# Thirty-six steps of unread identity products on TensorE, and a new written order, in a one-core gated-loop attention kernel with an MLP behind it

## The chip, the cores and the metric

The kernel runs on one core of one Trainium2 chip. The metric is the device time in microseconds of one execution. Inputs lie in the device's memory before the kernel starts, and the output is written there. The core has five engines that each execute their own instructions in order: TensorE (PE in the profile; its weight loads are counted apart, as PEld), VectorE (DVE), ScalarE (ACT), GpSimd (POOL) and SyncE (SP), which here only issues the transfers.

## The reference

Four batches, eight heads, 768 tokens, 48 channels. Each token decays a complex state per channel, adds an outer product of key and value, and is read with the query. The result is put side by side over the heads (3072 tokens of 384 values) and goes through an MLP of 2048 features with a parametric ReLU.

```
B, H, S, D = 4, 8, 768, 48
mag = sqrt(a_re*a_re + a_im*a_im);  scale = minimum(mag, 0.999) / (mag + 1e-6)
a_re_n, a_im_n = a_re*scale, a_im*scale
for t in range(S):
    new_re = ar*S_re - ai*S_im            # ar, ai: the gates of token t, per channel d
    new_im = ar*S_im + ai*S_re
    S_re, S_im = new_re + k[t,d]*v[t,e], new_im
    y[t] = einsum('d,de->e', q[t], S_re)
x = y as (3072, 384)
h = x @ w_in                              # 384 -> 2048
out = (maximum(h, 0) + alpha*minimum(h, 0)) @ w_out     # 2048 -> 384
```

All is 32-bit floating point, except that `w_in` and `w_out` arrive as 64-bit numbers and are turned into 32-bit ones on the chip.

## The kernel before

The tokens of one batch are cut into 6 chunks of 128, so there are 24 units of work (4 batches x 6 chunks), each for all eight heads. Around them stand the work that makes the gates, the loads, the conversion of the weights, and the MLP.

**Gates** (`gates`, nine groups: the first chunk of batch 0, its chunks 1 and 2, its chunks 3 to 5, and then two groups of three chunks for each other batch). A group computes the magnitude on ScalarE and VectorE (L269 to L291), the decay of each token (L380) and the products of decays over 2, 4, ... 64 tokens (L396). It then forms the running product of the unit complex numbers: inside runs of 8 tokens and inside 8 such runs (`product`, L416 and L418), across the runs (the chain over `run`, also L416 and L418, one small pair after the other), and back to all tokens (L474, L477, L485 to L489, then L504 and L507). ScalarE copies between these parts (`three`, L444 and L446). In every group but the first, an operation of at most 80 elements per partition goes to GpSimd, a larger one to VectorE; in the first group all of it is VectorE's. At the end, decays and phases go out to scratch memory (`decs`, `phs`).

**Weights** (`weights`, 16 pieces). For each, ScalarE makes three passes (L585, L587, L589), GpSimd one (L593), and VectorE two (L595, L597). There are two buffers `top` for the passes between, so L593 of one piece, L595 and L597 follow each other closely.

**Units** (`unit`). VectorE turns queries and keys by the phases (L739, L741), then goes through six levels of spans (1, 2, 4, 8, 16, 32 tokens) in three visits of two. In each level VectorE multiplies by decays (`step`, L794), ScalarE copies the keys and queries of the level (L817 into `WQ`, L833 into `W`), and TensorE forms the products of keys and queries (`meet`, L756, groups of 16 products of 96x32). VectorE (L779) or ScalarE (L770) masks them into `A`. Then TensorE transposes keys (L865), forms the states' additions (L877), and adds up `y` from `A` and the values (L897, two halves of two parts of three levels each); VectorE carries the states on (L907, L915; from unit 4 on ScalarE in L907's place), and TensorE adds the part that comes from the state (L927). ScalarE takes `y` out (L941), and it goes through scratch memory into the layout that the MLP wants (L946, L959).

**The MLP** (`all_mlp`; the last three groups of tokens by `late_features`, `mixes` and `late_outputs`, which use a scheme with seven products in place of eight). TensorE forms features (L975), ScalarE and VectorE apply the parametric ReLU (L982, L984), and TensorE adds up the outputs in the tile `ps_o` (L994).

**Buffers.** Tiles of one kind are used in turn: three of `KQ`, two of `T` and of `WQ`, one of `PP`, `V`, `W` and `run`; in TensorE's accumulator memory two of `lv` and `h`, one of `misc`, `y` and `o`.

**What sets the order.** Each of these parts is a Python generator that issues some instructions between two `yield`s. Each has a letter, in the order in which it is added: A to I the gate groups, J and L the loads, K the half rows of the values, M the weights' loads, N and O the conversion of `w_in` and `w_out`, P to Z and a to m the 24 units, n the load of x, o the MLP, p the mixes, q the late outputs. A written string of 4605 letters, `ORDER`, says which generator goes on by one step:

```
def run(self, order):
    for c in order:
        next(self.tasks[self.LETTERS.index(c)], None)
```

So the string sets the order of instructions in the queue of each engine, the DMA issues on SyncE's included, and nothing is reordered after that. What the generators yield (an engine, a cost, what it follows) was of use to the planner that found the string; here it does nothing. An engine waits at an instruction until the data and the buffer that it needs are there, and everything behind it in that engine's queue waits too.

Of the kernel before, what the change touches and what calls it, by code (L numbers as in the profile page):

```python
# [9 lines left out]
F32 = mybir.dt.float32  # L10
# [3 lines left out]
AF = mybir.ActivationFunctionType  # L14
ALU = mybir.AluOpType
PSUM = bass.MemoryType.PSUM
DRAM = bass.MemoryType.DRAM

P = 128
# [8 lines left out]


ORDER = (  # L30
    "AABBMMAAAAAAAAAAJAAJAJAAAAAABJAAAAAAAABMMMMAAAABLABAABAAABAKAABAAAANAKANALBOKABLBKANNAKABALBBAMABABO"
    "LAKABAAOOLAKABAAAMABALAABAKAAALABAALAABKANKAABAAAABAABABANBAANBABABAANAAAANNKAAAABABANMBNBNCOCNBJBNN"
    "JBJBOKBOBOBLNKOOBKBNBBCBOOBOPCBCPPLMBOCBCBBKBBMCBLBBKCBPBJPCPPPPPPCOONPMJOLPPBOJBPCBLBPJBCKPBPKBBBLB"
    "BKBBBBCCPBPNBPBBBOBBCCCPBCBPPBPBPOCKNNCMBBBBPBBPPOOBCBPNBCPMCPNPCNONCOCPNPJCOCPDNOPDJOJCCPCCPCOPLCLP"
    "PPCQLCLODLNCNDCDJQNCPDPLCDOMPDCQDJCJPDQQJNQKCJDCDPPMCNCCDCCCCDDQQCCCOnCCMQCLCCDDDKQLoOJoDCOOLKOCDQQN"
    "JOQLoMROLCOLQJOORKDLCoKCDooooCQCKCCRQCoQDCJRoooooRCOCQoLoQKCNCoQQQLCQCKQQQNKQRQJDNQKRoQooNQDRCCCCRDQ"
    "DQCQQQOCoRLCNLLQRRCoLQRDoRLCoLQQoMRoLNoCooCLoRoQooDQDQJCCCCooRLOCRLROoLoRoRCoROOCQLRRooooooCRQLRLooo"
    "oRCQoRLQRDCRKNoDNDNoooRNDRDJNNoEDoEDRJoRDJRooDJRoLoDoLoDSDRLooooooDJNDEJooooRSDDEDRRoRKDNDoRRoooJoES"
    "oDRERRnDSSRLoSooESJDSoSDKoODoSJDoLoooSODoLSSLoSDLoJSSDJoooooDDLSDDoLDEDLTooSoSoooDSSSSLoSDoSLETLDJSo"
    "ooooSoSLDooTDJSKooETDoJoSooTTDEEoDoSETKoSToTDSDooDDEooSDoDSSTSoELLSELooooSSSLoTELDDDDDoSLoooooETDJTo"  # L40
    "DSLSSooSToSoDoLooooEoDoooooJoTToDEJTDoELooooonTUoETLLooETKoooLTEToLTTooooToUJoTTTEJoooooETULoEJooooL"
    "UoEUDoEUTDDJooDoEooUoDooToTTDTDTTooLoLDoLoUULoooooDoUDLTULoooooUTLUELUoTTTooooJUUoTLTUoFTLEooooULEUo"
    "LUUTToTUULUooooELoEoUVFUUUooooUEoVVJUJoJEKoooooEUEUUUUUFUEoFUELULooEUJVFoJEoLVoJoUoooVLEoUFJoEUVUoVL"
    "FVLUEooooEoVVEEFVEJoVoooooEJVFEVLEVELonooooEoLVVEEJoVELLoooooEWVoEVLooEKoEVVEVoJEoWLoVLVVoooJoEWEoKF"
    "WoVooVWWoEVWoooEoLVKFFJoWWEVEWEFooooooVEWEVEEVEFFVVoWLEVoWoLWLoWLoEEEWEoVJoELWoLEVELooooEKoEoLWFFVWL"
    "VFoLVLVWWVLWVLooooWVFoVWEoVLoWFLoooWEFEoEEWoJWoEJoKFooWoEWoooEEWJoFEWWWWWELLoooEoWLoXWoJLXJoooooLXLo"
    "ooooFXJoooXFGXFLWWFWGXFoLWWoWJXoXFFFoXWWWLoooooXoFXFoXXooooFoXXoGXoGoooooFXXFoXoJXGFnooooLoXFXGoXLXo"
    "LXFLGLFoooXoXLoFJoXoFGooJFoJXoYJoGoJFXYFoFXFYXFoooFXFFXXYXGXFYLYJYFoooooYLoFYFoooLFXFXLYFXLoXYoLFZYF"
    "XLXYXoXYXFFoLFFYKYFFGFLGJooooooFJoYFGKoooooLFGZYFYJoKGFoJYYYYYJFYGLooooooFLZYFoLoooKZYFZYLZoLFZJooZY"
    "oJFGZYZFFFKoooooYGFYYYYYZYZGYLFZoLZLoLFooooLFoZFLoYGGZLFGLZLoLoooYYoZFaYLZYYooYoLGZoYYoZLoooZZaoZLZo"  # L50
    "LZoGJZoFZooFGonGZFFGoJZoJoFZoZFGZZZZooGLZLoZGGoLooLoFFoooLFoKooaoFaoooooFoZaLoGaZLaZLZJooZaoaLGoJZoa"
    "ZLoHoGaHGZLoooaaGoZaoJoLaaLGoaooooooooaoGaJHGLGHoooJoGoJHoGJaoaaGaaaaGoooaooGoHGaGooooHoGbGaoaobbJHG"
    "aaoaGHaGabGooaLGbLoGLoHoLbGoLbobaGaLbGLJbbGLooooGaGGbJGoaGJaoHLbGboLbaabLGHaKooooGbbGoaGLoGHGbGLoLHo"
    "ooGLbGbJGobGGJbobboJbHbbbKoGGGboooHHbGbcoooooboGJboJbcbbboLbJocbLooHLoLGobbGbJcHcLbcbnbcLHHGLoooooLc"
    "cGoLbcobHboooocdoHccJHoJcoGLGoooLoccoJHocJoJoooLcHdcHLooccGoLoGcooocLHcGcHccocodHocoGdcGoooooddcGGoG"
    "oGooooGoooocococJdccoKdLodcLoLodoLoHdooocoHdHdoHIoHIoLoooLccdLcKocHcoLddoLHoJcHcdIcooooooLHdcdLddodL"
    "dddHLIoooooLHoLddHJodooJHoIKoHdJHIodoHdoeHIdedIHddooLIHeJoHLdoIoLHoLoKHeoooHdenHoeHdLHeHoLJHdddoooHL"
    "eeHoLdooodeHLHoHoLHoIeHLeIeLHJHoHIJoooHoHeHooeeHHHHdeHddodILooooooIeLoeLJeeeIJooooeJoHIHeoJHHeoeefeH"
    "fHoooeoeooeoIHeeeoeefoLLoefLoIeoKofLIfJofHILHoooLoeIHoLfoHLefLeoLIooofKeJIfJeILoHooooffefeLoeoooeoff"
    "LooHLfoLIoooIfngfIoJIoJfffoHoJfffHHfJoofofooHofofoogoofHogHoIfKHgfooooIoHofffgHLgoLLIofLgfLLoooooogH"  # L60
    "oILgoooLoIoLgoLoILgJooogofgLfIgofLofLfoggoIfgffJofJoooooIoIgogJgggggJggoooJoIgJIogoIgogooIooIghIIgIg"
    "hhKJKgIggoLogILgIhoLIghIJggLgooohILoIIoJIoLIoIggIoohLIhIoILhIIogLohhIoILIIoLIoooIKIhIoJooiLhIhoJhooI"
    "JhIoLohLhoiooIhIiooooIIooooILhJhiihIJhhhJohoooJhhhIohoIhiIhoiIhihIhhhhihjoLhLiLLIhhhiLoooooIhoLioLih"
    "hiLhLooooIiiohoIiLoLjhLoooooiLIioLLiioiJiiJiooooiiIoiooIoooiIoiIoJoiIoioiiiiioLIiLoJojoLoIjJoooojoij"
    "iojLioJijjoLoijoiiiioooojJoLojLojooLjoJojLjoLojJoLoooJokoLoLjkojJooojjjjjjLonokLoJkJoJjjoooojpojojko"
    "kjokjjkjjjkjoLkjLoLooLokLoooLkjkLjkjLoLkkoLojkLojjLjojoookokookkkjoLoLokLoookkpkoookoJklJoookolkoopk"
    "okkkkkookLlLkoLooLokLoplJJLLoooooololJklkJJkooklLoklLookklokLolmJJoooooooLoooooooooomloloolLooLllLmL"
    "onlmoooooomomollolllllollmooomloploooooplolomoooomoolmolollllmLmoLmomomolomlolooommllmmollooomooollm"
    "ooomooooomoLoooLooomoLoLooplLLLooooLooooooooooolqoLmomoLoLoLopoooooooomooooooooooooooooooooomooooooo"
    "ooooooooomomomoomoomomoooomomomoqmqmqmmmqqmqnqqqqqqoqoooqoooooooqqoqqoooooooooooqoqqooqoqqqooooooooo"  # L70
    "oooqooqoqooooooooooooooooqqoqqqqoooooooooqoqqoqooqqoqooqoqoqqqooqqooqqoqooqqoqqqqoooqoqqoqooqoqooooq"
    "oqoqooqoqoqoooqqqoqqonooooooooooooqqooqqooooqooooooooooqqqooooqooqoooqoqqoqooqqoooooooooooooooqoqqoq"
    "oooooooooqqooooooooqqoqqoqooqoqoooooooqoqqooooooqoqqoqoooooooqoooooqqqoooooqoqqoqooqoqooqqoqoqqqoqoo"
    "ooqoqqoooooqoqqoqooqoqooqooqoqoqooqoqoqoooqqqoqqoooooooooooooooooqoqqoqoqqoqqooooooooooqqoooqooooqoq"
    "qoqqoooooooqooooooqooooqooooooooooooooqooqqqqooooooooooooooooooooooooooooooooooooooooqoqqoqoqoqooqqo"
    "qoqoqqqqqqqqqqqqqqqqqqqqqqqqqqqqqqqqqqqqqqq")


class Ring:
# [25 lines left out]
def kernel(  # L105
# [32 lines left out]
    nc = tc.nc  # L138
    B, HP, _, D, S = q.shape
    H = 2 * HP  # L140
    DM, DF = w_in.shape
# [17 lines left out]
    work = ctx.enter_context(tc.tile_pool(name="work", bufs=2))  # L159
    dram = ctx.enter_context(tc.tile_pool(name="dram", bufs=4, space=DRAM))  # L160
    ps = ctx.enter_context(tc.tile_pool(name="ps", bufs=1, space=PSUM))

# [5 lines left out]
    ident = consts.tile([P, P], F32, tag="ident")  # L168
# [370 lines left out]
    start = consts.tile([D2, B, H], F32, tag="start")  # L539
# [718 lines left out]
```

## The time and the profile before

| what | value |
|---|---|
| median of three runs | 841.18 us (837.4 to 842.11) |
| profiled execution, its own time | 835.86 us |
| span of the profile | 834.1 us |
| mean granted clock of TensorE | 0.967 |
| TensorE busy (products) | 685.3 us, 82%, 11680 records |
| VectorE busy | 678.7 us, 81% |
| ScalarE busy | 505.0 us, 61% |
| GpSimd busy | 322.7 us, 39% |
| chain that ended last, by engine | PE 56%, DVE 13%, POOL 10%, ACT 9%, DMA 7% |

The span runs from the first to the last record of the profile; the profiled execution's own time is 1.76 us longer. A 32-bit product on TensorE leaves two records, so 11680 records are 5840 products, and the records count as many weight loads. The granted clock is the share of full speed at which TensorE was allowed to run. Times of single instructions below are starts and durations of this one profiled execution, in us from the start of the span; behind an instruction, in square brackets, stands the time that its engine was idle before it and what ended that.

### The profile page before, as it was taken

The page shows a single profiled execution, that of the slowest core. Times are in us where ns is not written, and L with a number is a line of the kernel's source. Part 1 is how long each engine was busy: PE and PEld are TensorE (multiplying, and loading weights), DVE is VectorE, ACT ScalarE, POOL GpSimd, SP SyncE. Part 2 cuts the span into 40 slices and gives each one's busy share as a digit, 9 for nine tenths or more (in the row PEclk, how much of TensorE's full clock was granted, in tenths as well). Part 3 has the DMA queues.
Part 4 walks back from the last instruction along what each step waited for, and adds up shares of the span by engine and source line. Part 5 has one row for each costly group of instructions (what it writes and reads, how often), then busy time and mean ns, then how long its engine had stood idle before and what let it go on. Part 6 is the DMA issues. An engine that isn't in the chain of part 4 may idle for free.

```text
span 834.1 us, 27800 instructions
## 1 busy us (share of the span) xinstructions
PE 685.3 (82%) x11680; PEld 540.9 (65%) x11680; DVE 678.7 (81%) x1044; ACT 505.0 (61%) x1243; POOL 322.7 (39%) x448
## 2 busy tenths in 40 slices
PE   0001315869989989999989999999999999999997
PEld 0001304656767767777767777677677767899997
DVE  6987978999988899989979988996877875455574
ACT  8576777567666687775777598554656535312121
POOL 6288348558513800861463057007100000333333
PEclk9999855999999999999999999999999999999999
DMA  8594984695678568758866765777566531101000
GB/s 240 166 262 111 291 263 135 202 238 137 155 218 223 139 174 239 160 135 232 214 167 169 228 166 145 211 191 194 112 196 148 140 102 36 44 19 39 1 20 20
DMA packets 186597, 130.98 MB, mean 157 GB/s; under 512 B 74728, under 2 KB 176872, under 8 KB 186088
## 3 DMA queue, kind: packets, MB, share of 16 engines
q1 hardware_dynamic: 186472, 129.20, 57.3%
q8 instruction: 92, 1.51, 0.8%
q14 instruction: 33, 0.27, 0.1%
HBM read 100.82 MB, written 35.71 MB: 164 GB/s over the span
## 4 chain that ended last, share of the span: by engine, by line
PE 56%; DVE 13%; POOL 10%; ACT 9%; DMA 7%; issue 3%; SPq 1%; DVEq 0%; ACTq 0%; POOLq 0%
PE ps_o L994 15%; PE ps_h L975 15%; PE ps_m L1169 6%; POOL gate L416 4%; PE ps_lv L756 4%; PE ps_h L1094 3%; PE ps_y L1094 3%; PE ps_y L897 3%; DVE KQ L794 3%; POOL run L418 3%; PE ps_kv L877 2%; PE ps_y L927 2%; DVE gate L416 2%; DVE gate L504 1%; DMA T<-decs 1%
## 5 line engine op out<-in xcount | busy, mean ns | idle before, releaser
L975 PE MATMUL ps_h<-xT,w_in_sb 128*128 128x256 f32 (+1 forms) x960 | 228.7, 370 | 8.9 <-DMA xT<-ysc 6.2
L994 PE MATMUL ps_o<-w_out_sb,g_sb 128*128 128x384 f32 x576 | 221.8, 501 | 12.0 <-DVE g_sb L984 11.6
L975 PEld LDWEIGHTS ps_h<-xT,w_in_sb 128*128 128x128 f32 x960 | 172.5, 195 | 58.4 <-DMA xT<-ysc 6.3
L794 DVE TENSOR_TENSOR KQ<-KQ,T 96x1024 f32<-96x1024 f32 x120 | 148.4, 1237 | 24.1 <-PE ps_lv L756 12.6
L994 PEld LDWEIGHTS ps_o<-w_out_sb,g_sb 128*128 128x128 f32 x576 | 101.6, 190 | 55.2 <-DVE g_sb L984 14.0
L416 POOL TENSOR_TENSOR gate<-gate 128x72 f32<-128x72 f32 (+1 forms) x56 | 39.1, 699 | 168.3 <-ACT gate L446 163.7
L982 ACT ACTIVATE g_sb<-ps_h 128x256 f32<-128x256 f32 (+1 forms) x160 | 57.7, 360 | 74.3 <-PE ps_h L975 73.5
L1157 POOL TENSOR_TENSOR sums<-g_sb 128x128 f32<-128x128 f32 x48 | 21.3, 464 | 189.4 <-DVE g_sb L1138 189.4
L984 DVE SCALAR_TENSOR_TENSOR g_sb<-g_sb,al,ps_h 128x256 f32<-128x256 f32 (+1 forms) x160 | 71.2, 446 | 26.9 <-ACT g_sb L982 26.4
L756 PE MATMUL ps_lv<-WQ 96*32 96x32 f32 x2304 | 34.2, 203 | 61.1 <-DVE WQ L739 55.2
L756 PEld LDWEIGHTS ps_lv<-WQ 96*32 96x32 f32 x2304 | 26.2, 116 | 82.8 <-DVE WQ L739 55.3
L913 ACT ACTIVATE St<-St,T 96x48 f32<-96x48 f32 x288 | 68.6, 323 | 7.0 <-DVE St L915 6.9
L817 ACT COPY WQ<-KQ 96x1024 f32<-96x1024 f32 x48 | 50.1, 1044 | 23.3 <-DVE KQ L794 23.1
L396 POOL TENSOR_TENSOR gate<-gate 128x72 f32<-128x72 f32 (+5 forms) x24 | 25.3, 1056 | 67.5 <-DVE gate L396 66.4
L593 POOL TENSOR_SCALAR top<-top 128x768 f32<-128x768 f32 x16 | 41.2, 2582 | 19.6 <-ACT top L585 19.6
L756 PE MATMUL ps_lv<-KQ,W 96*32 96x32 f32 x1536 | 24.0, 203 | 29.5 <-ACT W L833 29.0
L416 DVE TENSOR_TENSOR gate<-gate 128x576 f32<-128x576 f32 (+3 forms) x70 | 47.3, 676 | 0.9
L897 PE MATMUL ps_y<-A,VL 64*48 64x64 f32 x2304 | 42.4, 223 | 5.7 <-issue 5.7
L833 ACT COPY W<-KQ 96x512 f32<-96x512 f32 x48 | 30.9, 643 | 26.4 <-DVE KQ L794 17.0
L770 ACT ACTIVATE A<-ps_lv,columns 128x64 f32<-128x64 f32 x144 | 38.7, 336 | 10.8 <-PE ps_lv L756 10.7
L504 DVE TENSOR_TENSOR gate<-gate 128x1152 f32<-128x1152 f32 (+2 forms) x36 | 44.2, 1253 | 0.1
L865 PE MATMUL ps_kt<-ident,KQ 96*128 96x96 f32 x192 | 25.7, 258 | 22.5 <-ACT T L868 17.0
(174 smaller groups left out, 1434.8 us busy)
## 6 DMA issues: line engine op xcount, KB each, us to landing
T<-decs SPq DMA_DIRECT2D x48, 384.0 KB
PP<-phs SPq DMA_DIRECT2D x24, 387.0 KB
KQ<-in_q_dram SPq DMA_DIRECT2D x48, 192.0 KB
decs<-gate SPq DMA_DIRECT2D x7, 1152.0 KB
phs<-gate SPq DMA_DIRECT2D x14, 576.0 KB
KQ<-in_k_dram SPq DMA_DIRECT2D x40, 192.0 KB
vsc<-in_v_dram SPq DMA_DIRECT2D x48, 144.0 KB
VL<-vsc SPq DMA_DIRECT2D x48, 144.0 KB
```

Of the source, the lines that this page charges most:

```text
L416: on(4 * k).tensor_tensor(out=m, in0=w[:, 1::-1].unsqueeze(2).to_broadcast([P, 2, 2, k]), in1=pairs_of(u), op=ALU.mult)
L504: TT(out=m[:, a], in0=U5[:, 1 + a], in1=turned(off3, o)[:, a].unsqueeze(1).unsqueeze(3).to_broadcast([P, L // 2, nb, 2]), op=ALU.mult)
L756: nc.tensor.matmul(t[64 * i + j:64 * i + j + HC // 2, p], lhsT=keys(n, g), rhs=queries(n, g), start=True, stop=True)
L794: nc.vector.tensor_tensor(out=x, in0=x if x0 is None else x0, in1=m, op=ALU.mult)
L817: nc.scalar.copy(z.rearrange("p i n t -> p i (n t)").rearrange("p i (m h) -> p m i h", h=h), bass.AP(tensor=KQ.tensor, offset=KQ.offset + ...
L897: nc.tensor.matmul(o, lhsT=Vp[h][64 * i:64 * i + 64, s, e_ * D:(e_ + 1) * D], rhs=a, start=False, stop=False)
L913: nc.scalar.activation(St[:, n], before[:, n], AF.Copy, scale=T[0:D2, n, TL - 4 + s:TL - 3 + s])
L975: nc.tensor.matmul(p, lhsT=w_in_sb[:, f // 2, kk, f % 2 * P:(f % 2 + 1) * P], rhs=x_of[m][:, kk], start=(kk == 0), stop=(kk == NK - 1))
L982: nc.scalar.activation(gt, p, AF.Relu, scale=-1.0)
L984: nc.vector.scalar_tensor_tensor(out=gt, in0=gt, scalar=al_1[:, f:f + 1], in1=p, op0=ALU.mult, op1=ALU.add)
L994: nc.tensor.matmul(sums[0], lhsT=gt[:, c * P:(c + 1) * P], rhs=w_out_sb[:, f], start=(f == 0), stop=(f == NF - 1))
L1094: nc.tensor.matmul(o, lhsT=lhs, rhs=rhs, start=(at in (0, 5)), stop=(at in (4, 8)))
```

## The change

Two things change. First, a generator `steady` is added, the last one, with the letter r. It takes the accumulator tile `ps_o` before the MLP's first output does, and goes through 36 steps of four products each, the 128x128 identity by itself, into the first 128 columns of that tile. Each product starts a new sum, and nobody reads the tile. After the last step the tile is free for the MLP.

Second, the string `ORDER` is another one: 4641 letters, the 36 for `steady` among them. The rest issues the same instructions as before, in another order. The diff, with only the first two lines and one further line of the string:

```
+STEADY = 36
...
 ORDER = (
-    "AABBMMAAAAAAAAAAJAAJAJAAAAAABJAAAAAAAABMMMMAAAABLABAABAAABAKAABAAAANAKANALBOKABLBKANNAKABALBBAMABABO"
-    "LAKABAAOOLAKABAAAMABALAABAKAAALABAALAABKANKAABAAAABAABABANBAANBABABAANAAAANNKAAAABABANMBNBNCOCNBJBNN"
...
+    "rAABBrMMrArJAArAAArAAArAArAAArAAAAABArAArAAAAABAMMJMJJArAArABrABALrKABrAANAArBAAAAArBAMAKOArBLrAKAAr"
+    "LBBBNKrALABBrLABBrLNNArKABOrKOOANLrAMNAAMBKAABAKBBALBABNAANBAAAAAABAOBAAAABAABABAABALANNAKAABMABALAB"
...
+    "PDODPOJCPCJrOOJrKPCrCCCCCCCPCCCLrODCLCPDLCNLDCQCDCJQDJLPDQCDMCOCQPPPQLCQNPCJPrNKDPJJDDrCPPMNQDCKPQNL"
...
+    def steady():
+
+        for i in range(STEADY):
+            e = yield PE(1.0, takes=() if i else (R["o"],))
+            if not i:
+                rest = ps.tile([P, DM], F32, tag="o", name="ps_o")
+            for j in range(4):
+                nc.tensor.matmul(rest[:, 0:P], lhsT=ident, rhs=ident, start=True, stop=True)
+        R["o"].put(e)
...
         plan.add(late_outputs())
+        plan.add(steady())
         plan.run(ORDER)
```

Where the new string puts things, as far as it matters here. In TensorE's queue 27 of the 36 steps stand at the head, before everything else. The other nine stand between the second half of unit 0's L897 and unit 2's first L756: two after the first three levels of that half, two ahead of L927, two after the first two L756 groups of unit 1, one after the third L975, one after the sixth, and one between the two first L756 groups of unit 2.

VectorE's queue has the same 108 instructions ahead of unit 0's L739 (place 109), and again the same instructions ahead of unit 2's L739 (place 179). Between these it differs most around the third gate group's inner products, seven pairs of L416 and L418. From place 141, before and after:

```
before  L597 L416 L907 L418 L416 L915 L418 L907 L416 L915 L418 L739 L416 L595 L595 L418 L597 L416 L741 L418
        L269 L416 L597 L418 L794 L416 L279 L418 L281 L289 L794 L779 L363 L363 L794 L380 L595 L597
after   L396 L416 L418 L416 L418 L416 L418 L907 L416 L418 L416 L595 L418 L416 L915 L418 L595 L416 L739 L418
        L269 L741 L907 L794 L597 L915 L597 L279 L281 L794 L779 L289 L363 L363 L794 L380 L595 L597
```

The last L595 of both rows is the eleventh of the kernel. In the queues of ScalarE, GpSimd and SyncE the same instructions as before stand in another order in many places.

More of the change, by code (lines that the diff above doesn't have):

```diff
@@ L30 @@
 ORDER = (
-    "AABBMMAAAAAAAAAAJAAJAJAAAAAABJAAAAAAAABMMMMAAAABLABAABAAABAKAABAAAANAKANALBOKABLBKANNAKABALBBAMABABO"
-    "LAKABAAOOLAKABAAAMABALAABAKAAALABAALAABKANKAABAAAABAABABANBAANBABABAANAAAANNKAAAABABANMBNBNCOCNBJBNN"
-    "JBJBOKBOBOBLNKOOBKBNBBCBOOBOPCBCPPLMBOCBCBBKBBMCBLBBKCBPBJPCPPPPPPCOONPMJOLPPBOJBPCBLBPJBCKPBPKBBBLB"
-    "BKBBBBCCPBPNBPBBBOBBCCCPBCBPPBPBPOCKNNCMBBBBPBBPPOOBCBPNBCPMCPNPCNONCOCPNPJCOCPDNOPDJOJCCPCCPCOPLCLP"
-    "PPCQLCLODLNCNDCDJQNCPDPLCDOMPDCQDJCJPDQQJNQKCJDCDPPMCNCCDCCCCDDQQCCCOnCCMQCLCCDDDKQLoOJoDCOOLKOCDQQN"
@@ L36 @@
[L36 to L75, printed above, removed]
@@ L76 @@
-    "qoqoqqqqqqqqqqqqqqqqqqqqqqqqqqqqqqqqqqqqqqq")
+    "rAABBrMMrArJAArAAArAAArAArAAArAAAAABArAArAAAAABAMMJMJJArAArABrABALrKABrAANAArBAAAAArBAMAKOArBLrAKAAr"
+    "LBBBNKrALABBrLABBrLNNArKABOrKOOANLrAMNAAMBKAABAKBBALBABNAANBAAAAAABAOBAAAABAABABAABALANNAKAABMABALAB"
+    "AABAAAAAAAAAAAOAKBONOBCNKOOCBNBJLNBBJNNBKBKBNBBOBNBCOBCBPBCBBOCBOPPJLLJKJCBJKPCBPKBKCKBBPPCMOOPMPMLP"
+    "BCBBPBBBCPBKKOPPCOPBPBPPBBBBBCCPBBBPBPBBBOBBCCCPBNCBBNBJOBBBPNNBCPMPPNLPPPBBOOKBCBCNBPMCCPOPCNOPNCNN"
+    "PDODPOJCPCJrOOJrKPCrCCCCCCCPCCCLrODCLCPDLCNLDCQCDCJQDJLPDQCDMCOCQPPPQLCQNPCJPrNKDPJJDDrCPPMNQDCKPQNL"
@@ new lines @@
+    "COMCLCQCCDDCCDDDQOnDJOOJQQNOLQLOoJoLRDOCoLrOQLCOOKRLCoLQQKCoooorMCDQCJKDRQCKQKNRRrJoCDoCNJCRoQQQQCQo"
+    "QoQoDQCoQRCDCooooQQCDRCQCDCROoNRQQoQooRCCCDCQQORLDQRCoLRoCoLCoNooLoQoCoLRRCDQQQKCRQCoCLoooooRoQRCCNN"
+    "LoooLCooMRRRRoRRQRQCLLooRoRoooRCCRLCLLooooooLCLoooooCDQNQKDNNNDODoOoooooRDEoNNEDooooJRDOOJoNRJoDJooD"
+    "oooNRoDoooRRDoLoERLDLRDJERRJDoSDLoooRoRDEDSDRRJRSDLERSSLSKoESDSSRDnODJESDLLOSSLESJDSDoLLoooSSDJoDoDJ"
+    "SDoLooLSToDSLLSDooooDSDJSSDoTSJSSJoooooSoSDTJDETooSooTSToSEEoSETDEooooDToDSDoDTDDDDSDSSEoESoLTLoooLo"
@@ new lines @@
+    "TooLoEooLToDDLSooTLSSELSLoSoSoTSSSLDDDDooooooSoLDoooEDLooJTToEEDKoooooTDLoEJoooooLoTUDKTnDEoooLTooJT"
+    "DTJEoTTDoooooTUTToTEooooToEUoEToooooUUEoEUEDDDoooooDoooToDToDTJTTToDLoLoLUoLDoooooDTLUUoTJooooULoLTT"
+    "TULEUTUoTUTJLoooooEFUULoTUFLoooooULEoUTooEoUUUUUUoToLELoUUVUEoooUoUoEJFVVoJEJoooooUoEJUUJEUEUUJFooLE"
+    "oLUoFEoLUEoUVEUJEooUoLVEUooFVVUULVoUVFLELooooLoEVVEKEoVFEJnoooooVEVLWFEVLVJoEKoooooLEVVEJEoVELKooooo"
+    "VEoVLEVVVEVEVVVooooLEoWLEVJVWJEoJoooooWEJWFEoKWVKooEFFVEoFooooWEVFWVFEoWoooVEWEVVVoXLEoKoVLEELWoLEEV"
@@ new lines @@
+    "EooooWLEWoLEoLEFFWLEWLoEWLoooooEVoLVEWELVKVFWoWLVVEWWWWLWEVooooWVoWEVWLoFoWJooooJFFWEoooEWFoooWEEJFW"
+    "WWEWWoLoXJoLoWLEWKooooooEXLoLoooXXWLoXFWJXWooLWWoFGoFGXXFLFoFXLWJoooooXoFFXLoXFJooXoLoXoXoFLGXoFWWKo"
+    "ooooGoFLXXFoGFWoooFoLXoooGXLXnFGJFJXooooooXFXJoXXFXJooooGYJooJXFoGoooYXooFoGFXFoFXYFXXXXooFYLXFLGGoF"
+    "LYXYLYFJLoFXFoooXXoYYFLFXFYXFoXXXoooooFYXoZFKGYYLYFFoLFGFLooooFYFoJYFoFLFFoFYJFLoooooJFGFYLYoLYFoLYY"
+    "LGoooFJZooJYoYYZJYYKoYKoooGZZJFFZYGoYoFFFoZYFoYoZYFYYYZYoGLYLoZLoGoLFoYZFLYaGFYLFZLoZYZLYYLooooLZZoo"
@@ new lines @@
+    "YYLZGYLFoLGoooZZaLoLJZZoooooZJZGZZJZoooZoFZGKooFZFFoJZFoooooFZGZFGZaGZZoFLGLoaLoooZFoLoGoLaFoaLLoooa"
+    "FoLoaaonZLoaoooooaGaZaoGaoHooooaaLooaJHGLZZZaaJGZLaZaoZaGaZZLaooooooZaGJoaGGGooaoaoHooooGLaGJoHGoooo"
+    "GooGbGGoGaoooobbJJJHoGoaoHaaaoaaGoGbLHGJboLoaobLoHLGbGbLaGobGHaLLbbGLoooGHGaoJaoaaaobJGaLHLKGGGbGoGH"
+    "GooobboGJGobGLoJbbLGoGLbGKoooLGoGLGoGJoJbobHooKbJobbbocbHooHbbbobooocGGbGoGbcooooJHGbJHobGbbbbooLGcb"
+    "noHKbooLoLHccGLoGbLGobLHHGcbLobKbobbbcLcodoboGHcoJdcJHoooooccKocooooccooGcGoLoHLJooocHcKoccccocJoLdo"
@@ new lines @@
+    "LccoooLdoHLcHoHLcHoHGGGoJooocGocooGcGocGccccdoLdGoLLodGoLddoooocLoHcLdLJoooooodHIcoLooodHLdcIdLcoLHo"
+    "ddJoHLccoLdccccHHLoooooododLIHooHoIdoJoodJedoJIoooJHodJIoddoJoHdddoooIHdHodoeoIdHJeKdIddHIHoHeooooHI"
+    "oHoddeLHeHILdHeHLoLdfKLoooHodddHooooeeHLHIHeLHLoeoooooeLHIIeLoLdeoLdHLooooeeoLoHdeHIHoHddLHoooeeHdoH"
+    "eeeHeoeeoIoeeJeoooJHIHeoeooHHeoHHoHIeeeeeHIHeoHLIHfJoHenooLfoHLLfLoHIoooofJefLHIHJHJeHfLeoJeoLfoLfoo"
+    "oIoHefoeoeeLHIoefHoooHfIofIoofILooJfIoLfoooLgoJoofLLoJooogJofJfonfffoIoHffffgoofofooofHogfooooHggfgf"
@@ new lines @@
+    "fffoLoLoLHHgHgoooofHJoLogLoHfgLoooooLIogKogfLgLIfffJooooLggoLgoLooooIgogIfoofILfoffogofgKgoooghgoLgg"
+    "ogJhogKohoogoIgKIoJoIoJIgoJgIgIgggooLILIoJoIohLIoIgJIhoILLoooghgIJIhLgIhgoILghIgogoghLoIhIoooLIIohIo"
+    "JoJihILoLoohhoIhLIoIILoohLhILIiIohIooooooIoIooIoIiIhohoohiIJohohJhihIoJIihohhJiohJoIIihophoohoIIIihI"
+    "hihhhILooLoihLojhoLoLiiLohhIhLiIhLhoooLiiIoLIohiLhoLoIhooohiLioLiiiioiLiojoJIiiiIoooIIoJioiIooIooiiI"
+    "iIiJiioJioLjioLoJILjLooooooJioLIoooojojLijIiLjjLLijiioooooLoooojjijoJjLoLojjioooLojoioLLooojpjoJJooJ"
@@ new lines @@
+    "ojjjjjjjJoJnoooookojokjooojkojoopkkokjjkjjkkkoooooojjkjkLopkjLLLLjjjkjJjjjjoooooojkkJokooooooooLkkJk"
+    "kkkLkkkLoJooooooLkoJkooLloLkokLloLoLooooJloJoJollLolJooloooooooolkkkkkklkmkoLloLoLoklLooomLooLllLklk"
+    "okpokkkkkoooooLlloloJooolJoloollLooLoLlooollLllloLloLoomLooooooomooommlmoloooooomoooloolllllmoLLomLo"
+    "olLolLLLolnmooooooLmomolmlolmlolmoloooomoooolooLooLooomoLmoLopLLlnoooooooooooommmmoqmomomooooooooooo"
+    "ooooooooomomooooooomomopooooooooooooooooooooomomomoomoomomoooomopmomoqmqmqmmmqqmqqqqoooqoqqqqqqooqoo"
@@ new lines @@
+    "qqoooqoqqoqqooqoqooqoqooooqoqqqooooooqoooooooooooooooooooqoqqooooooooooooooooooqonqqqoqooqoqooqoqoqq"
+    "qqqqqqqoqqoqoooooooooqoqqoqooqoqooooqoqoqooqoqoqoooqqqoqqoooooooooooooooqoqooqoqoqqoqqoooooooooooooo"
+    "oooqoqqoqooqoqooqqoooooooqqoqoqqoooqoqqqoqooqoooooooqooqqoqqoooooqooooooooooqooooooooqooooooooooooqo"
+    "qqoqqoqoooooqoqqoqooqoqqooqoqoqqqqoooooooooooqqoqqoqooqoqooqoqoqoqoqooqoqoqoooqqqoqqoooooooooooooqqo"
+    "qooooqoqqoooooooooooqqooqoqooqoooqoqqoqqoooooooooooooooooqoqqoqooqoooooooqoooooqqoooqoqooooooooooooo"
@@ L79 @@
+    "oooooqoqqoqooqqoooooooqqoqooqooqoooqoqqqoqqoqooqoqoqqoqqqqqqqqqqqqqqqqqqqqqqqqq")
 class Ring:
```

## The prediction

> **What bounds the kernel now.** I read the page's slices first, then the table of stretches, then the timelines of the engines in the stretch that stood out. In the slices each digit is a fortieth of the span, 20.9 us.
>
> ```profile
> PE   0001315869989989999989999999999999999997
> DVE  6987978999988899989979988996877875455574
> PEclk9999855999999999999999999999999999999999
> ```
>
> TensorE (PE) is nearly unused for the first 100 us and full from about 190 us on; VectorE (DVE) is full from 20 to about 330 us. So there are two stages: a run-up that VectorE sets, and a long stage that TensorE sets. The stretches say it in numbers (length, then busy us of PE, PEld, DVE, ACT, POOL, then the granted clock).
>
> ```profile
> 100.00:110.00 10.00, 0.14 (x12) 0.01 (x1) 9.71 (x15) 7.24 (x10) 0.00 (x0) 0.50 0.94 299
> 120.00:130.00 10.00, 2.67 (x40) 2.31 (x40) 4.30 (x4) 3.28 (x7) 8.40 (x14) 0.50 0.61 189
> 150.00:200.00 50.00, 38.05 (x710) 28.80 (x712) 49.02 (x67) 32.00 (x72) 30.23 (x28) 0.97 0.82 224
> 300.00:400.00 100.00, 97.38 (x1781) 72.85 (x1782) 93.30 (x120) 70.84 (x187) 36.80 (x43) 1.00 0.74 200
> ```
>
> From 150 to 200 VectorE works 49.02 of 50 us, and from 300 TensorE over 97 of 100. A microsecond won on VectorE before 150 therefore arrives whole at the end. Two idle stretches of VectorE stand there:
>
> ```profile
> 79.98 1.69 DVE L380 SCALAR_TENSOR_TENSOR gate<-gate 128x1152 f32<-128x1152 f32 x1 [5.72 <-ACT gate L291]
> 126.74 1.22 DVE L595 TENSOR_SCALAR top<-top 128x768 uint32<-128x768 uint32 x1 [5.57 <-POOL top L593]
> ```
>
> Behind both stands GpSimd (POOL). Its own rows, with start, duration and the wait before:
>
> ```profile
> 66.50 5.38 POOL L418 TENSOR_TENSOR run<-gate 128x6 f32<-128x6 f32 x1
> ...
> 113.72 0.57 POOL L416 TENSOR_TENSOR gate<-gate 128x72 f32<-128x72 f32 x1 [16.03 <-ACT gate L446]
> 114.37 1.74 POOL L418 TENSOR_TENSOR gate<-gate 128x36 f32<-128x36 f32 x1
> 116.18 1.31 POOL L416 TENSOR_TENSOR gate<-gate 128x72 f32<-128x72 f32 x1
> 117.57 1.26 POOL L418 TENSOR_TENSOR gate<-gate 128x36 f32<-128x36 f32 x1
> 118.91 2.45 POOL L416 TENSOR_TENSOR gate<-gate 128x72 f32<-128x72 f32 x1
> 121.43 0.26 POOL L418 TENSOR_TENSOR gate<-gate 128x36 f32<-128x36 f32 x1
> ```
>
> The same L418 takes 5.38 us while VectorE is full and 0.20 us at 74.70, when it is idle; in the chain of the third gate group the ops take 1.3 to 2.5 us until VectorE runs dry at 121.17, then 0.26 to 0.32. So GpSimd waits for VectorE, and VectorE later waits for GpSimd.
>
> **Profiled run and median.** The profiled execution took 835.86 us (span 834.1, 1.76 outside it); the median of the three runs is 841.18, 5.3 above. I make the sum against the profiled execution and take the same difference off the median. What this kernel's measurement can tell from no change is about 0.5%, 4.2 us.
>
> **The 27 steps at the head.** In TensorE's queue 27 of the 36 steps (108 products) stand before anything else and wait only for the identity, whose last GpSimd op ends at 1.6 us. Their price is bounded by the 128x128 products of L975 (two records each): eight records took 2.08 us at 127.13 with the clock at 0.50, six took 0.83 at 170.45 with it at 1.00. A step costs 2.08 or 1.11 us, the 27 cost 56.2 or 29.9, and end at 57.8 or 31.5. TensorE's first work of before starts at 52.62 and its second waits until 59.28 for ScalarE. At the high end the first multiply is 5.2 us late and still ends (58.5) ahead of the second. Cost 0, hidden by the 52.62 us of idle time.
>
> **The nine other steps** (36 products, 10.0 to 18.7 us) stand between unit 0's L897 and unit 2's first multiplies, about 91 to 130 us. From 90 to 130 TensorE idles 29.3 of 40 us. Queued behind them are L927, which waits for VectorE's L915; the L756 multiplies, which wait for ScalarE's copies; one feature and one L756, which may be ready. I take +0.3, with ends 0 and 4.2 (two steps at 2.08).
>
> **The clock.** The 9s of PEclk before 83 us are no full clock: the 32-column L756 takes 244 ns from 60 to 70 us and 199 from 300 to 400, and the first change on record comes near 94. Between 141.6 and 148.4 it is at 0.50 again. What VectorE loses to slow products in the run-up is its wait for TensorE, 1.3 us in all. I take −0.6 (0 to −1.3), since after the nine steps TensorE's queue has the same dips. The head burst ends at least 15 us before the first real product if it gets the full clock, so nothing of it can be left. [...]
>
> **The order, 50 to 80 us.** VectorE's list has the same 108 instructions ahead of unit 0's L739 in both. The last L507 of the first gate group stands 1.7 us of work later, so the phases leave later; in exchange a 768 KB weight load stands ahead of them instead of behind. The second half of the T load is now issued behind two small loads, a 144 KB vsc copy and St; its reader L794 starts at 55.58 and may come up to 1.7 later, of which part fits into the 1.88 us idle before L279. ScalarE's copies L444 and L446 for the run products stand ahead of two copies, so GpSimd's run chain starts about 2 us sooner and the 5.72 us idle shrinks by about 1. I take −0.5 (−1.5 to +1.7).
>
> **The order, 90 to 127 us.** In before the third gate group's seven pairs L416/L418 on VectorE are interleaved with two L597, L741, L269, L794, L915, L279; they run from 91.8 to 111.4. Now the last pair stands behind 11.7 us of work: seven pairs of 0.74+0.45, L739 1.21, and four short ops of 0.55. With −0.5 they run from 91.3 to 103.0. ScalarE's L444 follows, L446 now stands behind L272 and L274 (1.17 each, after VectorE's L269 at 104.3) instead of behind four others, and ends at 107.0 instead of 113.7. VectorE's next 16 instructions are 17.0 us by their rows, to 120.0, and then comes the same L595 (the eleventh), which needs GpSimd's eleventh L593, now after 13 chain ops instead of 14.
>
> Thirteen ops from 107.0: at the rate of 113.72 to 121.43 (five ops, 1.54 us each) 8.5 are done at 120.0, the other 4.5 take 0.37 each, L593 2.1: L595 at 123.8. At the rate of the second group's chain, 48.65 to 58.63 (14 ops, 0.71), all is done before 120.0. So L595 starts between 120.0 and 123.8, against 126.74. I take a middle rate of 1.1: 11.8 done at 120.0, 0.4 and 2.1 more, 122.5, that is −4.2 (−2.9 to −6.7), the −0.5 included. [...]
>
> **After 130 us** unit 2's L739 is again at the same place in both lists (row 179), later units stand a few rows earlier or later in turn, and the last quarter differs in details. TensorE's waits after 200 us sum to 12.8 us, so little can be won; I take 0 (−6 to +3).
>
> Sum: 0 + 0.3 − 0.6 − 4.2 + 0 = −4.5: profiled 831.4, median 836.7.
>
> **Rivals.**
> - The nine steps are not hidden. Place: TensorE's queue, 91 to 130 us, at half clock, 2.08 us each. If five of them (those between features and multiplies, and those ahead of units 0's and 1's next work) stand before items that are ready, they cost 10.4; with −4.2, 847.4. It decides from the third step on the path. For it: products at 0.50, VectorE full and waiting for the L756 results; against: 29.3 us idle there.
> - The gain becomes a wait of ScalarE. GpSimd's seventh L418 now stands behind two L593, and ScalarE's in-order L444 (124.65 in before) waits for it, with L982 and the next copies behind. One L593 took 6.49 us at 157.33 under a full VectorE; with two slow ones L444 comes at 131, L982 at 133 as in before (133.24), and nothing is won: 841.
> - More than forecast: the chain gets the fast rate, L595 starts at 120.0 (−6.7), and the clock holds (−1.3): 833.5. [...]
> - That the 36 steps do nothing for the time is part of the forecast.
>
> **Chances.** Forecast 0.36, steps on the path 0.28 (their places are those where TensorE and VectorE hand each other work), gain lost 0.20, more 0.16. The forecast lies at the bound of 4.2, a little over half of it beyond: 0.23 + 0.16 = 0.39 faster; 0.13 + 0.20 = 0.33 same; 0.28 slower. The range reaches to 848, past the first rival, and down to 828, 5 below the last; it leaves out the last part of the −6 after 200 us and of the steps' full price.
>
> **What would show it.** Right: GpSimd's third chain starts near 106, VectorE's idle time before the eleventh L595 is under 4 us, L756 has its first record near 52 and 240 ns. Wrong: L595 not before 126; a long ScalarE wait for L418 near 125; TensorE's steps with VectorE idle behind an L756; TensorE waits after 200 us well over 13 us; a clock at 1.00 throughout from 95.

## The result and the profile after

| | before | changed |
|---|---|---|
| median of 20 runs each | 837.92 us (833.32 to 845.36) | 843.92 us (839.57 to 850.43) |
| profiled execution, span | 835.86 us, 834.1 | 844.57 us, 842.9 |
| mean granted clock | 0.967 | 0.935 |

The changed kernel takes 1.0069 of the time before (95% interval 1.0042 to 1.0097): slower by 6 us, where I had forecast faster by 4.5. In this section and the next, all line numbers of changed kernels are one higher than before's up to L1201, so L757 is before's L756; L1208 is the product of a step. (A correction to the section on the kernel: the two strings have 4543 and 4579 letters, not 4605 and 4641.)

The slices of the changed kernel, a fortieth of 842.9 us each:

```profile
PE   9301537768988999899999989999999999999997
DVE  6987989998978899699899978988789565546574
PEclk9755658978999999999999999999999999999999
```

The 27 steps fill TensorE's first slice, and the clock reads 5 to 7 tenths from the second to the sixth slice and stays below full in eight slices. The same four stretches as before (PE, PEld, DVE, ACT, POOL, then the clock):

```profile
100.00:110.00 10.00, 1.75 (x48) 1.40 (x48) 9.57 (x14) 6.64 (x8) 0.65 (x1) 0.59 1.11 308
120.00:130.00 10.00, 4.94 (x56) 4.81 (x57) 6.10 (x7) 4.96 (x7) 8.61 (x12) 0.55 0.93 279
150.00:200.00 50.00, 37.30 (x775) 28.62 (x773) 48.76 (x67) 34.02 (x73) 29.05 (x28) 0.90 0.88 224
300.00:400.00 100.00, 96.28 (x1771) 71.55 (x1760) 89.77 (x113) 70.66 (x185) 32.71 (x44) 0.98 0.70 183
```

Up to 200 us little has changed; in the stage that TensorE sets, it works 96.28 of 100 us in place of 97.38. The two waits of VectorE that the prediction went by:

```profile
79.95 1.36 DVE L381 SCALAR_TENSOR_TENSOR gate<-gate 128x1152 f32<-128x1152 f32 x1 [5.94 <-ACT gate L292]
126.42 1.17 DVE L596 TENSOR_SCALAR top<-top 128x768 uint32<-128x768 uint32 x1 [3.76 <-POOL top L594]
```

and the end of GpSimd's third chain:

```profile
109.35 0.97 POOL L417 TENSOR_TENSOR gate<-gate 128x72 f32<-128x72 f32 x1 [10.87 <-ACT gate L447]
...
123.98 0.32 POOL L417 TENSOR_TENSOR gate<-gate 128x72 f32<-128x72 f32 x1
```

Both L380 and L595 of before stand within 0.4 us of where they stood (79.98 and 126.74). Unit 4's second phase multiply, at the end of the run-up, starts at 194.3 us in the changed kernel and at 194.4 before. So the 8.8 us between the two spans arise after that. There TensorE's table of waits (200 to 760 us: line, what it waited for, sum, times, longest) reads, before and changed:

```profile
PE ps_y L897 <- issue: 2.0, 3, 1.1
PE ps_y L927 <- issue: 0.5, 1, 0.5
```

```profile
PE ps_y L898 <- issue: 5.7, 4, 2.9
...
PE ps_h L976 <- issue: 3.2, 2, 1.9
...
PE ps_lv L757 <- issue: 1.1, 1, 1.1
...
PE ps_kv L878 <- issue: 0.8, 1, 0.8
```

"issue" is time in which TensorE waits for nothing that the profile shows, no data, no buffer and no other engine: 2.5 us before, 10.8 now. My prediction had read the 2.5 us as part of a sum and not asked what sets it.

### The profile page after: what moved, and what is told of

It is laid out like the page before. It is cut to its first block, busy times and chain, and to the rows that moved or that the text cites. A ratio compares the mean times of both kernels' runs of the same rounds, so it can differ in the third digit from the quotient of the medians.

```text
span 842.9 us, 28388 instructions
## 1 busy us (share of the span) xinstructions
PE 722.7 (86%) x11968; PEld 577.7 (69%) x11968; DVE 680.1 (81%) x1044; ACT 505.0 (60%) x1243; POOL 329.2 (39%) x448
## 4 chain that ended last, share of the span: by engine, by line
PE 63%; DVE 14%; DMA 6%; ACT 5%; SPq 5%; issue 4%; POOL 4%; DVEq 0%; POOLq 0%; ACTq 0%
PE ps_o L995 18%; PE ps_h L976 17%; PE ps_m L1170 6%; PE ps_lv L757 4%; PE ps_y L898 4%; PE ps_y L1095 3%; PE ps_h L1095 3%; PE ps_kv L878 3%; DVE KQ L795 2%; SPq L702 2%; PE ps_y L928 2%; POOL gate L417 2%; DVE gate L505 2%; DMA VL<-in_v_dram 1%; PE ps_kt L866 1%
## 5 line engine op out<-in xcount | busy, mean ns | idle before, releaser
L995 PE MATMUL ps_o<-w_out_sb,g_sb 128*128 128x384 f32 x576 | 223.9, 505 | 9.0 <-DVE g_sb L985 8.9
L976 PE MATMUL ps_h<-xT,w_in_sb 128*128 128x256 f32 (+1 forms) x960 | 225.9, 367 | 4.5 <-issue 3.2
L995 PEld LDWEIGHTS ps_o<-w_out_sb,g_sb 128*128 128x128 f32 x576 | 102.4, 192 | 50.2 <-DVE g_sb L985 10.4
L985 DVE SCALAR_TENSOR_TENSOR g_sb<-g_sb,al,ps_h 128x256 f32<-128x256 f32 (+1 forms) x160 | 71.4, 446 | 23.3 <-ACT g_sb L983 22.9
L757 PEld LDWEIGHTS ps_lv<-WQ 96*32 96x32 f32 x2304 | 26.2, 115 | 66.1 <-DVE WQ L740 29.5
L757 PE MATMUL ps_lv<-WQ 96*32 96x32 f32 x2304 | 34.4, 202 | 43.1 <-DVE WQ L740 28.9
L397 POOL TENSOR_TENSOR gate<-gate 128x72 f32<-128x72 f32 (+5 forms) x24 | 30.2, 1260 | 61.9 <-DVE gate L397 54.9
L594 POOL TENSOR_SCALAR top<-top 128x768 f32<-128x768 f32 x16 | 38.3, 2397 | 26.2 <-ACT top L586 26.2
L898 PEld LDWEIGHTS ps_y<-A,VL 64*48 64x48 f32 x2304 | 40.3, 126 | 9.5 <-issue 8.9
L417 POOL TENSOR_TENSOR gate<-run,runs 128x12 f32<-128x12 f32 x46 | 38.4, 835 | 16.9 <-ACT runs L447 13.7
L757 PE MATMUL ps_lv<-KQ,W 96*32 96x32 f32 x1536 | 24.4, 205 | 23.3 <-ACT W L834 23.0
L419 POOL TENSOR_TENSOR gate<-gate 128x36 f32<-128x36 f32 (+1 forms) x56 | 42.1, 752 | 4.2
```

The lines of the kernel that those rows point to most:

```text
L417: on(4 * k).tensor_tensor(out=m, in0=w[:, 1::-1].unsqueeze(2).to_broadcast([P, 2, 2, k]), in1=pairs_of(u), op=ALU.mult)
L757: nc.tensor.matmul(t[64 * i + j:64 * i + j + HC // 2, p], lhsT=keys(n, g), rhs=queries(n, g), start=True, stop=True)
L898: nc.tensor.matmul(o, lhsT=Vp[h][64 * i:64 * i + 64, s, e_ * D:(e_ + 1) * D], rhs=a, start=False, stop=False)
L976: nc.tensor.matmul(p, lhsT=w_in_sb[:, f // 2, kk, f % 2 * P:(f % 2 + 1) * P], rhs=x_of[m][:, kk], start=(kk == 0), stop=(kk == NK - 1))
L985: nc.vector.scalar_tensor_tensor(out=gt, in0=gt, scalar=al_1[:, f:f + 1], in1=p, op0=ALU.mult, op1=ALU.add)
L995: nc.tensor.matmul(sums[0], lhsT=gt[:, c * P:(c + 1) * P], rhs=w_out_sb[:, f], start=(f == 0), stop=(f == NF - 1))
```

## The experiments

Strings are put together from the old and the new one. "Late" is what follows unit 4's first phase multiply in a string; where the first part of one order is followed by the other's late part, each generator goes on from where it stands. Every step is four products, and a product is four instructions on TensorE (two records of a product, two of a weight load), so the change's 36 steps add 576 instructions. All ratios are to the kernel before on the same chip, five rounds each, with 95% intervals.

**First four: steps or order, early or late.** Theory A and C put the loss into the order, late or early; theory B into the steps.

```
 e1:  ORDER = new without its 36 r                       (order alone)
 e2:  ORDER = 27 r + old with the other 9 r at the same neighbours
 e3:  ORDER = old up to unit 4 + new, late, no r
 e4:  ORDER = new with its 36 r up to unit 4 + old, late
```

> The new order with the 36 steps taken out of it. Theory A (the loss is made by the new order after 190 us, where the decays' store of the fourth gate group waits 3.5 us longer for GpSimd and the phases behind it in SyncE's queue are 5.35 us late): as slow as the change, 1.007 (1.004 to 1.010) of before. Theory B (the loss is made by the 36 steps, by their own time and by the clock that they pull to a half from 33 to 95 us): 1.000 or below, 0.995 to 1.002. Theory C (the loss is made by the new order before 190 us): as A. Granted clock: near 0.967 if the steps set it, near 0.935 if the order does.

> The old order with the 36 steps put into TensorE's queue at the same places (27 at the head, nine behind the same neighbours, the last one ahead of the first output). Theory A and theory C: 1.000 of before (0.997 to 1.003). Theory B: 1.007. Granted clock near 0.935 if the steps set it.

> The old order up to unit 4's first phase multiply (190 us), then the new one, no steps. Theory A: 1.007. Theories B and C: 1.000 (0.996 to 1.003).

> The new order with its 36 steps up to unit 4's first phase multiply, then the old one. Theory A: 1.000 (0.996 to 1.003). Theories B and C: 1.007 (1.004 to 1.010).

Measured: e1 1.0194 (1.0164 to 1.0224), e2 1.0230 (1.0183 to 1.0277), e3 1.0179 (1.0138 to 1.0221), e4 1.0288 (1.0257 to 1.0320). All three theories miss. The order alone is slow, the steps alone are slow, and both together are faster than either; half of one order with half of the other is slow as well. The waits on issue after unit 4 say where: 14.8, 20.9, 13.7 and 21.7 us. In e2 the late part is the old order, instruction by instruction; yet:

```profile
PE ps_lv L757 <- issue: 8.7, 4, 3.0
PE ps_y L898 <- issue: 7.3, 5, 3.0
PE ps_y L928 <- issue: 2.7, 2, 1.4
PE ps_o L995 <- issue: 2.2, 1, 2.2
```

Here is the same work of TensorE in both, from the timeline (start, duration, engine, line, operation, count of records). Before:

```profile
336.88 0.43 PE L897 MATMUL ps_y<-A,VL 64*48 64x64 f32 x15
337.90 0.70 PE L897 MATMUL ps_y<-A,VL 64*48 64x64 f32 x33 [0.58 <-issue]
338.53 0.46 PE L756 MATMUL ps_lv<-WQ 96*32 96x32 f32 x32
338.80 0.49 PE L756 MATMUL ps_lv<-KQ,W 96*32 96x32 f32 x32
339.22 1.56 PE L975 MATMUL ps_h<-xT,w_in_sb 128*128 128x256 f32 x6
340.62 1.45 PE L994 MATMUL ps_o<-w_out_sb,g_sb 128*128 128x384 f32 x4
342.00 0.81 PE L927 MATMUL ps_y<-KQ,St 96*48 96x64 f32 x21
343.27 0.54 PE L927 MATMUL ps_y<-KQ,St 96*48 96x64 f32 x11 [0.45 <-issue]
```

Between the two waits lie 33 + 32 + 32 + 6 + 4 + 21 = 128 records of products and as many of weight loads: 256 instructions. In e2:

```profile
342.64 0.89 PE L898 MATMUL ps_y<-A,VL 64*48 64x64 f32 x48
343.46 0.46 PE L757 MATMUL ps_lv<-WQ 96*32 96x32 f32 x32
343.74 0.47 PE L757 MATMUL ps_lv<-KQ,W 96*32 96x32 f32 x31
347.26 0.21 PE L757 MATMUL ps_lv<-KQ,W 96*32 96x32 f32 x1 [3.05 <-issue]
```

Against before's first wait (behind 15 of the 48 records of L897) this one is 33 + 32 + 31 = 96 records or 192 instructions later, and 192 = 256 − 64, with 576 = 2·256 + 64. So the waits sit on borders of blocks of 256 instructions, and the steps at the head of the queue push these borders through all the work behind them. The page of before has a DMA queue that fits:

```profile
q8 instruction: 92, 1.51, 0.8%
```

92 packets of 16384 bytes; TensorE's 23360 records of products and weight loads are 254 for each. The changed kernel, with two and a quarter blocks more, has 94. From these counts I take the packets of q8 for TensorE's own code.

The traces bear this out far beyond these few waits. In the sixteen profiles of this document TensorE has 152 waits on issue. Counted with the semaphore instructions that the traces list for TensorE, 151 of them stand at one and the same place modulo 256, to within two instructions, and each of the 151 ended 1.2 to 1.8 us after a packet of q8 had landed. About one border in ten has such a wait.

The load of a block starts mostly 0.5 to 3 us after TensorE enters the block ahead of it (median 1.2 us before, 1.5 in the changed kernel), and takes about 1 us (before's 92 loads 0.88 to 1.94, median 1.08). Where TensorE has run through the block ahead before the load has landed and those 1.2 to 1.8 us have passed, it waits at the border. In the changed kernel's wait that ends at 344.17 us TensorE was through with its block at 341.25; the load started at 341.41, 6.3 us after the block was entered, took 1.25 us, and the wait ended 1.5 us after it had landed. There are two ways to that. In e2 seven waits stood behind blocks of small products that had taken 1.9 to 2.3 us, and six behind blocks of 2.8 to 4.8 us, where the next load had started 1.4 to 4.6 us after the block was entered. The eight waits of the changed kernel after unit 4 are all of the second kind: blocks of 3.6 to 6.1 us, with the next load 2.0 to 6.3 us after the entry.

Most borders cost nothing that the trace shows: in e2 about 80 of 94 have no wait on issue. The others cost up to 3.05 us each, and 20.9 us in sum after unit 4.

**Next four: theory D, blocks of 256.** Only the number of steps at the head is changed.

```
 e5:  STEADY = 32;  ORDER = 32 r + old                   (512 instructions)
 e6:  STEADY = 4;   ORDER = 4 r + old                    (64)
 e7:  STEADY = 4;   ORDER = 4 r + new without its 36 r   (64)
 e8:  STEADY = 48;  ORDER = 12 r + new                   (768)
```

> The old order with 32 steps of four products (128 products, 512 instructions on TensorE) ahead of everything else in its queue. Theory D (TensorE's code comes in loads of 16 KB, 256 instructions; where a block of 256 falls on nothing but small products it is run through in 1 to 2 us, and the next block is not there yet: waits put down to issue; what counts is the number of added instructions modulo 256): 512 is two whole blocks, so as before, 1.000 (0.997 to 1.003), waits on issue after 200 us 2 to 4 us. Theory B (the steps' work and the clock they pull down cost the time): 1.015 to 1.023. Theory E (any stir of the run-up upsets a tuned order): 1.015 to 1.025.

> The old order with only 4 steps (16 products, 64 instructions) ahead of everything else, 3 to 5 us of work in an idle time of 52 us. Theory D: shifted by 64 as with the 36 steps, 1.022 (1.018 to 1.028), waits on issue after 200 us 15 to 24 us. Theory B: 1.000 (0.998 to 1.003). Theory E: 1.000 to 1.005.

> The new order with 4 steps (64 instructions) at the head in place of the 36. Theory D: at the offset that the new order was found with, so as the change, 1.007 (1.002 to 1.010), well under the 1.019 of the new order alone. Theory B: 1.019 (the steps that are left are a ninth). Theory F (the 36 steps help by their work, by the clock or by delay): 1.016 to 1.020.

> The change with 12 more steps at the head (48 products, 192 instructions): 768 added instructions in all, three whole blocks. Theory D: as the new order alone, 1.019 (1.014 to 1.025). Theories B and F: as the change, 1.005 to 1.010; the 39 steps at the head take about 38 us of the 52 us before TensorE's first work.

Measured: e5 1.0003 (0.9978 to 1.0028), e6 1.0207 (1.0158 to 1.0257), e7 1.0052 (1.0019 to 1.0085), e8 1.0145 (1.0097 to 1.0193). Theory D holds in the times of all four (e5's waits on issue, 4.7 us, are a little over the 2 to 4 expected). 128 products ahead of the old order cost nothing; 16 products, by the rate of the changed kernel's 27 steps an estimated 3.9 us of work in an idle time of 52, cost 2%. In e5 the waits sit where they sat before, behind the 15th of 48 and the 21st of 32 records:

```profile
343.55 0.67 PE L898 MATMUL ps_y<-A,VL 64*48 64x64 f32 x33 [0.47 <-issue]
...
348.92 0.54 PE L928 MATMUL ps_y<-KQ,St 96*48 96x64 f32 x11 [0.48 <-issue]
```

And the new order is as good with 16 products as with 144 (1.0052 against 1.0069, intervals overlapping), so what it draws from its 36 steps is their number modulo 64 products, not their work or the clock.

**What is left: where are the 0.7%?** Two runs put the halves together again, now with the borders where the late half wants them; two move eight issues in SyncE's queue that stood ahead of unit 6's phases, for which VectorE waits 4.8 us in the changed kernel and 2.2 before.

```
 e9:   STEADY = 4;  ORDER = 4 r + old up to unit 4 + new, late
 e10:  ORDER = new without r up to unit 4 + old, late
 e13:  ORDER = change, eight L (loads of unit 5's values) behind the J that issues unit 6's phases
 e14:  the same move in the old string
```

> The old order up to unit 4's first phase multiply (190 us), then the new one, with 4 steps (64 instructions) at the head, so that the code blocks stand as the new order wants them. If what is left of the loss lies in the new order's part after 190 us (phases of unit 6 late behind SyncE's queue): 1.005 (1.002 to 1.009). If it lies in the part before: 1.000 (0.997 to 1.003). If blocks are not what made the earlier run of the same two halves slow (1.018): 1.018 again.

> The new order up to unit 4's first phase multiply, then the old one, without steps, so that the blocks stand as the old order wants them. If the loss lies after 190 us: 1.000 (0.997 to 1.003). If before: 1.005. If blocks are not what made the earlier run of the same two halves with 36 steps slow (1.029): 1.02 or more.

> The change with one thing moved, in SyncE's queue alone: eight issues for the values of unit 5 (V and VL) go behind the load of unit 6's phases, which stood behind them at 248.4 us. If that queue makes the wait of 4.8 us of VectorE for the phases and the 4.5 us of TensorE at 254.7 us, these fall under 2.5 and 2 us and the time by 2 to 5 us, to 1.001 to 1.005 of before. If another thing is next (the phases' own store, the decays' load behind it), 1.007 as the change.

> The kernel before with the same move: eight issues for the values of unit 5 behind unit 6's phases. The wait for the phases there is 2.2 us, and TensorE idles 1.5 us at 249 us: 0.998 to 1.000 of before; if the values come too late for that, 1.000 to 1.004.

Measured: e9 1.0075 (1.0041 to 1.0109), e10 0.9994 (0.9972 to 1.0016), e13 1.0081 (1.0052 to 1.0110), e14 1.0036 (1.0011 to 1.0061). The loss lies in the late part; the new run-up is as good as the old one. With the borders put right, the same halves that took 1.018 and 1.029 take 1.0075 and 0.9994 (the 1.029 run had the steps too, which e5 shows to be free). Moving the phases wins nothing: issued at 246.0 us in place of 248.4, they shorten VectorE's wait for them to 3.2 us, but then the values come late. TensorE's waits from 192 to 300 us in e13:

```profile
PE ps_y L898 <- DMA VL<-vsc: 3.8, 1, 3.8
PE ps_o L995 <- DVE g_sb L985: 3.2, 3, 2.7
```

In place of 5.5 us for L985 in the changed kernel: one wait was traded for another.

What differs is again issue. From unit 4's second phase multiply to the end, one profile each:

| late part, borders | runs | rest of span, us | waits on issue | all waits of TensorE |
|---|---|---|---|---|
| old, +0 | before, e5, e10, e14 | 639.7, 642.2, 641.3, 639.6 | 2.5, 4.7, 0.2, 0.7 | 13.4, 16.8, 14.1, 14.7 |
| new, +64 | change, e7, e9, e13 | 648.6, 648.3, 643.6, 649.5 | 10.8, 6.6, 7.3, 8.3 | 21.6, 22.8, 18.1, 22.0 |
| new, +0 | e1, e3, e8 | 661.8, 654.7, 660.2 | 14.8, 13.7, 14.5 | 27.8, 25.9, 24.7 |
| old, +64 | e2, e4 | 661.6, 662.3 | 20.9, 21.7 | 29.0, 29.0 |

The profiled execution of e6 (old, +64) was the longest of its six, 870.1 us against a median of 860.6, and is left out of the table; it has 23.1 us of waits on issue.

Means of the first two rows: 640.7 and 647.5 us, 6.8 apart; waits on issue 2.0 and 8.3, 6.2 apart; TensorE's other waits 12.7 and 12.9. So the new order, at the place it was written with, still waits 6.2 us longer for its code, about the whole of what it loses. This is read from sums of single profiles; no run took these waits away. Much of it is one border: all four profiles of the second row wait 2.5 to 3.5 us there, behind a block of 6 us, where the next load began 6.1 to 7.0 us after the block was entered. In the changed kernel:

```profile
344.17 1.94 PE L898 MATMUL ps_y<-A,VL 64*48 64x64 f32 x59 [2.92 <-issue]
346.05 2.25 PE L995 MATMUL ps_o<-w_out_sb,g_sb 128*128 128x384 f32 x4
```

The lower rows lose some more than their waits on issue. A part may be the clock: behind the wait shown it reads half from 344.1 to 347.5 us, and the four records of L995 take 2.25 us, where before's at 340.62 took 1.45.

**Two more: the borders alone, by a little.**

```
 e12:  STEADY = 35;  ORDER = new with one r fewer at the head    (560, +48)
 e15:  STEADY = 34;  ORDER = new with two r fewer at the head    (544, +32)
```

> The change with one step fewer at the head: 560 added instructions, 48 modulo 256 in place of 64. From the trace of the change, with the block borders moved by 16 instructions, the time by which blocks are run through in under 4.5 us sums to 4.9 us after 185 us in place of 7.6, and under 5.5 us to 14.5 in place of 23.7. If the loss that is left (1.007) is waits on issue: 1.002 to 1.006, waits on issue after 192 us 4 to 8 us. If it is something else in the new order: 1.007 again with fewer waits on issue.

> The change with two steps fewer at the head: 544 added instructions, 32 modulo 256. By the same sums 6.1 us (under 4.5 us) and 14.8 (under 5.5): between the change and 35 steps, 1.003 to 1.007.

Measured: e12 1.0049 (1.0021 to 1.0077), 10.5 us of issue; e15 1.0154 (1.0114 to 1.0194), 12.3 us. e12's time fits what was expected, but it can't be told from the change, and its waits are above the 4 to 8 us expected, so it doesn't show that fewer waits on issue win back the 0.7%. e15 is a miss: my sum over the blocks of the change's trace ranked it close to e12. In its profile a block that is run through in 2.08 us ends at 471.96 with a wait of 1.08 behind it, where the change's block there took 3.62 and had none. The sum gets the broad valley right (a shift by 192 or 64 leaves it), not places inside it, where it also counts how late each load starts. No variant beats the kernel before; e10 equals it.

## Why the prediction was wrong

**Right: the 27 steps at the head.** Estimated at 29.9 to 56.2 us, hidden; they took 26.52 us from 1.64 on, a little under the low end, and TensorE's first real product started at 54.01. That their work is free is shown by e5.

**Right, within what was bounded: the nine others.** Taken at +0.3. Unit 2's phase multiply starts at 128.60 and was forecast to be unmoved; e7, without them, gives the change's time within the intervals. The rival that put five of them on the path (847.4) named a time near the one measured by luck: the cause was another.

**The order from 50 to 80 us: no gain.** Taken at −0.5, with VectorE's 5.72 us of idle time ahead of L380 about 1 shorter. That idle time was 5.94, and L380 started at 79.95 in place of 79.98.

**The clock: no effect.** Taken at −0.6. The clock read lower, and it cost nothing: e5's mean is 0.926 at 1.0003 of before's time. The gains of a held clock did not come either.

**Wrong: L595 at 122.5, a gain of 4.2.** It stands at 126.42. The place to look was right, the start and the length of GpSimd's chain were mis-sized. I had VectorE's seven pairs run from 91.3 to 103.0; they ran from 92.88 to 105.27. So ScalarE's L446 ended at 109.27, not 107.0, and the 13 GpSimd operations took 14.95 us (13.4 by my rates) and ended at 124.3 in place of 120.4: 2.3 us of that are the start, 1.6 the length. VectorE came to the wait at 122.7 in place of 120.0. The result is that of the rival in which nothing is won, but ScalarE's wait for the seventh L418 was not needed for it. e10 confirms it: the new run-up in place of the old makes 0.9994.

**The step that failed: "After 130 us … I take 0 (−6 to +3)".** It measured +8.9 in the two profiles (639.7 to 648.6) and 6.8 in the means of four. I had compared the orders by which instruction stands ahead of which, and reasoned from the sum of TensorE's waits. But the same instructions at the same places relative to each other are not the same queue: their place in the stream, counted from its start, decides which 256 share a code block. The edit adds 576 instructions at and near the front of TensorE's queue. That alone would have cost the old order 2.3% (e2); the new order, written with them in place, wins most of that back and remains 6 us short. None of my rivals had this mechanism. Its row was on the page ("q8 instruction") and in the waits ("issue"). Of my signs of being wrong, "TensorE waits after 200 us well over 13 us" came true with 20.8, and "L595 not before 126" with 126.42.

Two things stay open. What a border cost in these profiles follows from when its load started and how long the block ahead ran; why one load starts later than another was not tried. In e2's wait of 3.05 the code load began only 3.5 us after TensorE had entered the block, and the DMA share of the stretch from 340 to 344 us read 1.16; that the load queued behind data is argued, not shown. And beyond the border at 344 us, which pieces of the new late order cost it its 6.2 us of issue was not taken apart.

## What to carry to other kernels

In a long unrolled program, count the instructions that an edit adds ahead of work that is tight, modulo the size of a code block (here 256 on TensorE, 64 products in 32-bit): a harmless pad can move every border behind it (64 instructions in e6: 1.0207), and a control with a pad of whole blocks tells that from the pad's own work in one run (512 in e5: 1.0003). Look for the waits put down to issue and ask which block of instructions they end. Blocks that are run through fast are where a border hurt: of the 151 waits 148 stood behind blocks of 1.9 to 6.1 us, the shortest of them nothing but small products, while the median block of before took 7.0 us after 200 us. Of the places tried, each order here ran best at the one it was written with or 16 instructions from it, so half of one order with half of another says nothing until the borders are put back.

## What the hardware showed beyond that

The clock's record says less than it seems. From 60 to 70 us the small product (L756) takes 244 ns a record before and 244 in the changed kernel, with the record at 1.00 in the first and at 0.50 in the second (e5, too, has 244); from 300 to 400 us before, at 1.00, it takes 199. So from 60 to 70 us before's products ran as at the half clock, though the record reads 1.00 up to its first change at 93.8. And behind the burst of 26.5 us of dense products at the start the clock did not stay up: it reads 0.50 from 33.5 us on, 5.3 us after the burst's end, and TensorE's next product, at 54.0, came at 0.50.
